# x + alpha * fx: flat chunks instead of partition-major rows, and a first store that waits for an addition

## The chip, the cores and the metric

The kernel runs on one core of a Trainium2 chip. The metric is device time in microseconds of one execution, lower is better. The core has a VectorE (DVE in the profile) that does all the arithmetic here, a SyncE (SP) that issues DMA transfers in order, and 16 DMA engines that carry them out. On-chip memory (SBUF) has 128 partitions; HBM is the memory outside.

## The reference

```python
# x, fx: (512, 32, 640) bfloat16; alpha: (1,) bfloat16
def reference(x, fx, alpha):
    return x + alpha * fx
```

There are 10,485,760 elements in each of x, fx and out, 20.97 MB each, so 62.92 MB must cross between HBM and SBUF: 41.94 in and 20.97 out.

## The kernel before

Each tensor is seen as 128 rows, one for each partition, of 81,920 elements (160 KiB) that lie together in HBM. A row is counted in 160 units of 512 elements (1 KiB). A transfer takes a range of units of all 128 rows.

There is one buffer, `buf`, of 207 units a partition, too small for x and fx together (320). The tables `F` and `X` say at which unit of `buf` a piece of fx or of x lies: `(64, 96, 160)` in `F` puts the units 64 to 96 of fx at place 160. Places are used again: an addition overwrites x with the sum, after which the place of its fx is free for a later load. So a load waits for the additions that free its place, and these wait for earlier loads.

The order is written out by hand in `PLAN`, one step a line, and a loop at the end (lines 128 to 131) walks through it:

- `f i` and `x i` load a piece of fx or x (`load_f`, line 88; `load_x`, line 92), issued on SP;
- `a` brings alpha to all partitions (`alpha_to_lanes`, lines 110 to 118): a two-byte load, a matmul with ones, a copy;
- `m a b` multiplies units a to b of fx by alpha in place (`multiply`, line 97, VectorE);
- `t a b` adds: x becomes x + alpha * fx in place (`total`, line 104, VectorE);
- `s i` stores a piece (`store`, line 108), issued on SP.

Each engine takes its steps in the order of the plan. Waits between engines are put in where places of `buf` overlap, and a step that waits holds up what follows on its own engine. All transfers go through one queue, SP's, and the 16 DMA engines carry them out in that order. The first store comes last but two in the plan, but depends only on additions of units 0 to 64, long done when SP reaches it; so it is issued directly behind the last load of x (`x 3`). At the end (lines 133 to 135) SP waits for everything but the last store, and the program's end for that one.

Of the kernel before, what the change touches and what calls it, by code (L numbers as in the profile page):

```python
# [1 line left out]

# [4 lines left out]

ACT = mybir.ActivationFunctionType
ALU = mybir.AluOpType
F32 = mybir.dt.float32  # L10
BF16 = mybir.dt.bfloat16

K = 512
P = 128


F = [(0, 8, 96), (8, 64, 104), (64, 96, 160), (96, 128, 128), (128, 160, 175)]
X = [(0, 64, 0), (64, 96, 64), (96, 128, 96), (128, 160, 143)]
S = [(0, 64), (64, 128), (128, 160)]
N = 160  # L20
ALL = 207

PLAN = """
f 0
f 1
a
x 0
f 2
x 1
m 0 64  # L30
t 32 64
t 0 32
f 3
x 2
m 64 96
t 79 96
f 4
t 64 79
m 96 128
t 111 128  # L40
x 3
t 96 111
m 128 160
t 128 160
s 0
s 1
s 2
"""


@with_exitstack
def kernel(
    ctx: ExitStack,
    tc: tile.TileContext,
    x: bass.AP,
    fx: bass.AP,
    alpha: bass.AP,
    out: bass.AP,
):
    nc = tc.nc  # L60
    xv = x.flatten_outer_dims().rearrange("(p n) d -> p (n d)", p=P)
    fxv = fx.flatten_outer_dims().rearrange("(p n) d -> p (n d)", p=P)
    ov = out.flatten_outer_dims().rearrange("(p n) d -> p (n d)", p=P)
    assert xv.shape[1] == N * K

    consts = ctx.enter_context(tc.tile_pool(name="consts", bufs=1))
    psum = ctx.enter_context(tc.tile_pool(name="psum", bufs=1, space=bass.MemoryType.PSUM))
    whole = ctx.enter_context(tc.tile_pool(name="whole", bufs=1))
    ctx.enter_context(tc.manual_schedule())

    sync = mybir.DependencyInfo(mybir.DependencyClass.Sync, mybir.DependencyReason.DATA)
    buf = whole.tile([P, ALL * K], x.dtype, name="buf")
    done = []
    lanes = {}

    def units(v, a, b):
        return v[:, a * K : b * K]

    def at(pieces, a, b):

        s, _, h = next(p for p in pieces if p[0] <= a < p[1])
        e, _, g = next(p for p in pieces if p[0] < b <= p[1])
        assert h - s == g - e
        return units(buf, a + h - s, b + h - s)

    def load_f(i):
        a, b, _ = F[i]
        done.append(nc.sync.dma_start(out=at(F, a, b), in_=units(fxv, a, b)))  # L88

    def load_x(i):  # L90
        a, b, _ = X[i]
        done.append(nc.sync.dma_start(out=at(X, a, b), in_=units(xv, a, b)))

    def multiply(a, b):
        term = at(F, a, b)
        done.append(
            nc.vector.tensor_scalar(  # L97
                out=term, in0=term, scalar1=lanes["a_f"][:], scalar2=None, op0=ALU.mult
            )
        )  # L100

    def total(a, b):
        s = at(X, a, b)
        done.append(nc.vector.tensor_tensor(out=s, in0=s, in1=at(F, a, b), op=ALU.add))  # L104

    def store(i):
        a, b = S[i]
        done.append(nc.sync.dma_start(out=units(ov, a, b), in_=at(X, a, b)))

    def alpha_to_lanes():  # L110
        a_1 = consts.tile([1, 1], alpha.dtype, name="a_1")
        done.append(nc.sync.dma_start(out=a_1[:], in_=alpha[None, :]))  # L112
        ones = consts.tile([1, P], alpha.dtype, name="ones")
        nc.vector.memset(ones[:], 1.0)  # L114
        a_ps = psum.tile([P, 1], F32, name="a_ps")
        done.append(nc.tensor.matmul(a_ps[:], ones[:], a_1[:], start=True, stop=True))  # L116
        lanes["a_f"] = consts.tile([P, 1], F32, name="a_f")
        nc.vector.tensor_copy(out=lanes["a_f"][:], in_=a_ps[:])  # L118

    does = {  # L120
        "f": load_f,
        "x": load_x,
        "a": alpha_to_lanes,
        "m": multiply,
        "t": total,
        "s": store,
    }
    for step in PLAN.split("\n"):
        if step:
            what, *of = step.split()  # L130
            does[what](*map(int, of))

    rest = nc.sync.nop(nofuse=True)
    for i in done[:-1]:
        tc.add_manual_dep(rest.ins, i.ins.name, sync, reason="all but the last store")


# [1 line left out]
_INS = ['x', 'fx', 'alpha']  # L139
_OUTS = [((512, 32, 640), 'bfloat16')]  # L140


# [23 lines left out]
```

## Time and profile before

| | |
|---|---|
| median of 3 runs | 151.65 us (151.59 to 151.67) |
| the profiled execution | 151.67 us, of which the span from its first to its last instruction is 149.9 us |
| VectorE busy | 65.9 us, 13 instructions |
| DMA engines | 62.92 MB, 420 GB/s over the span, packets take 98.0% of it |

A page gives one execution. "q1 hardware_dynamic" is the queue that SP fills; the share beside it is the time that its packets took, of 16 engines' span. A row of a group of instructions reads: line, engine, operation, output and inputs with their shapes, count, busy time, mean ns of one, idle time before and what ended it. A row of a stretch reads: from and to in us, its length, busy time of each engine (with the count of instructions), the clock granted to TensorE, the DMA engines' mean share, and GB/s. A row of the timeline reads: start, length in us, engine, line, operation; instructions of one kind are merged, and "SPq" marks the issue of a transfer by SP, not the transfer.

### The profile page before, as it was taken

The page shows a single profiled execution, that of the slowest core. Times are in us where ns is not written, and L with a number is a line of the kernel's source. Part 1 is how long each engine was busy: PE and PEld are TensorE (multiplying, and loading weights), DVE is VectorE, ACT ScalarE, POOL GpSimd, SP SyncE. Part 2 cuts the span into 40 slices and gives each one's busy share as a digit, 9 for nine tenths or more (in the row PEclk, how much of TensorE's full clock was granted, in tenths as well). Part 3 has the DMA queues.
Part 4 walks back from the last instruction along what each step waited for, and adds up shares of the span by engine and source line. Part 5 has one row for each costly group of instructions (what it writes and reads, how often), then busy time and mean ns, then how long its engine had stood idle before and what let it go on. Part 6 is the DMA issues. An engine that isn't in the chain of part 4 may idle for free.

```text
span 149.9 us, 84 instructions
## 1 busy us (share of the span) xinstructions
PE 0.2 (0%) x1; PEld 0.1 (0%) x1; DVE 65.9 (44%) x13; POOL 0.2 (0%) x4
## 2 busy tenths in 40 slices
PE   0000000000000000000000000000000000000000
PEld 0000000000000000000000000000000000000000
DVE  0000009930079999999954998309920000000000
POOL 0000000000000000000000000000000000000000
DMA  5979996969899999999999999998998969697994
GB/s 164 606 337 398 490 525 280 560 280 560 376 437 437 428 420 420 420 420 420 428 463 463 437 437 428 420 420 367 472 490 350 560 280 560 280 560 315 455 446 184
DMA packets 1730, 62.92 MB, mean 420 GB/s; under 512 B 194, under 2 KB 194, under 8 KB 194
## 3 DMA queue, kind: packets, MB, share of 16 engines
q1 hardware_dynamic: 1730, 62.92, 98.0%
HBM read 41.94 MB, written 20.97 MB: 420 GB/s over the span
## 4 chain that ended last, share of the span: by engine, by line
DMA 51%; DVE 20%; SPq 1%; issue 0%; DVEq 0%
DMA buf<-in_x_dram 51%; DVE buf L104 20%; SPq L88 1%; SPq L112 0%; DVEq L104 0%
## 5 line engine op out<-in xcount | busy, mean ns | idle before, releaser
L104 DVE TENSOR_TENSOR buf<-buf 128x16384 bf16<-128x16384 bf16 (+2 forms) x7 | 43.5, 6251 | 20.5 <-DMA buf<-in_x_dram 20.5
L97 DVE TENSOR_SCALAR buf<-buf,a_f 128x16384 bf16<-128x16384 bf16 (+1 forms) x4 | 22.2, 5550 | 0.9 <-DMA buf<-in_fx_dram 0.9
L118 DVE COPY a_f<-a_ps 128x1 f32<-128x1 f32 x1 | 0.2, 157 | 21.5 <-PE a_ps L116 21.5
L114 DVE MEMSET ones<- 1x128 bf16 x1 | 0.2, 165 | 0.8 <-PEq L150 0.8
L116 PE MATMUL a_ps<-a,ones 1*128 1x1 bf16 x1 | 0.2, 158 | 22.3 <-DMA a<-in_alpha_dram 22.3
L150 POOL MEMSET const-bfloat16-1.0<- 128x1 bf16 x1 | 0.1, 101 | 0.0
L150 POOL MEMSET const-uint8-127<- 128x1 uint8 x1 | 0.1, 101 | 0.0
L150 POOL MEMSET const-float32-0.0<- 128x1 f32 x1 | 0.1, 98 | 0.2 <-issue 0.2
L150 POOL MEMSET const-float32-1.0<- 128x1 f32 x1 | 0.1, 98 | 0.0
L116 PEld LDWEIGHTS <-ones 1*128 1x128 bf16 x1 | 0.1, 97 | 1.0 <-DVE ones L114 1.0
## 6 DMA issues: line engine op xcount, KB each, us to landing
buf<-in_fx_dram SPq DMA_DIRECT2D x3, 4096.0 KB, 22.0
buf<-in_x_dram SPq DMA_DIRECT2D x3, 4096.0 KB, 21.4
buf<-in_fx_dram SPq DMA_DIRECT2D x1, 7168.0 KB, 21.4
out_dram<-buf SPq DMA_DIRECT2D x1, 4096.0 KB, 39.5
buf<-in_fx_dram SPq DMA_DIRECT2D x1, 1024.0 KB, 4.9
out_dram<-buf SPq DMA_DIRECT2D x2, 49.8
a<-in_alpha_dram SPq DMA_DIRECT2D x1, 0.0 KB
buf<-in_x_dram SPq DMA_DIRECT2D x1, 39.9
```

Source lines behind the costliest of these rows:

```text
L88: done.append(nc.sync.dma_start(out=at(F, a, b), in_=units(fxv, a, b)))
L97: nc.vector.tensor_scalar(out=term, in0=term, scalar1=lanes["a_f"][:], scalar2=None, op0=ALU.mult)
L104: done.append(nc.vector.tensor_tensor(out=s, in0=s, in1=at(F, a, b), op=ALU.add))
L114: nc.vector.memset(ones[:], 1.0)
L116: done.append(nc.tensor.matmul(a_ps[:], ones[:], a_1[:], start=True, stop=True))
L118: nc.vector.tensor_copy(out=lanes["a_f"][:], in_=a_ps[:])
L150: nc = _bacc.Bacc("TRN2", target_bir_lowering=False, num_devices=1)
```

## The change

The unit becomes 128 elements (`K = 128`). Each tensor is now flat and cut into three chunks of 254, 253 and 133 units a partition: a chunk is a contiguous stretch of HBM, within which each partition has a contiguous row of 63.5, 63.25 or 33.25 KiB (`rows` finds a range of units in its chunk). The table entries, the loads and the stores follow the chunks. fx of the first chunk comes in two loads (8 and 55.5 KiB a partition), x of the second in two (the later units first), so there are 8 loads and 3 stores where there were 9 and 3. `buf` keeps its size: 828 units of 128 elements, 207 KiB.

The additions are cut to fit: 8 of them and 3 multiplications, where there were 7 and 4. The last units of the second chunk that are not yet added, 254 to 309, are now added after the last multiplication, in two steps, 254 to 306 and 306 to 309.

`LATE` is new: the store `s 0 254` gets a wait for the addition `t 254 306`, with which it shares no data. SP issues it once that addition is done. The steps of the plan are now told by their units instead of by a number, and `said` keeps the instruction of each step so that the wait can be attached.

```diff
-K = 512
+K = 128
 P = 128
 
-F = [(0, 8, 96), (8, 64, 104), (64, 96, 160), (96, 128, 128), (128, 160, 175)]
-X = [(0, 64, 0), (64, 96, 64), (96, 128, 96), (128, 160, 143)]
-S = [(0, 64), (64, 128), (128, 160)]
-N = 160
-ALL = 207
+CHUNKS = [(0, 254), (254, 507), (507, 640)]
+
+F = [(0, 254, 507), (254, 507, 254), (507, 640, 442)]
+X = [(0, 254, 0), (254, 507, 575), (507, 640, 309)]
+ALL = 828
 
 PLAN = """
-f 0
-f 1
+f 0 32
+f 32 254
 a
-x 0
-f 2
-x 1
-m 0 64
-t 32 64
-t 0 32
-f 3
-x 2
-m 64 96
-t 79 96
-f 4
-t 64 79
-m 96 128
-t 111 128
-x 3
-t 96 111
-m 128 160
-t 128 160
-s 0
-s 1
-s 2
+x 0 254
+f 254 507
+m 0 254
+t 127 254
+x 380 507
+t 0 127
+x 254 380
+m 254 507
+t 442 507
+f 507 640
+t 380 442
+t 309 380
+x 507 640
+m 507 640
+t 254 306
+t 306 309
+s 0 254
+t 507 640
+s 254 507
+s 507 640
 """
+LATE = {"s 0 254": "t 254 306"}
 
 
 @with_exitstack
...
     out: bass.AP,
 ):
     nc = tc.nc
-    xv = x.flatten_outer_dims().rearrange("(p n) d -> p (n d)", p=P)
-    fxv = fx.flatten_outer_dims().rearrange("(p n) d -> p (n d)", p=P)
-    ov = out.flatten_outer_dims().rearrange("(p n) d -> p (n d)", p=P)
-    assert xv.shape[1] == N * K
+
+    def rows(t, a, b):
+
+        flat = t.rearrange("b s d -> (b s d)")
+        s, e = next(c for c in CHUNKS if c[0] <= a and b <= c[1])
+        v = flat[s * K * P : e * K * P].rearrange("(p n) -> p n", p=P)
+        return v[:, (a - s) * K : (b - s) * K]
 
...
+    said = {}
...
     def at(pieces, a, b):
 
         s, _, h = next(p for p in pieces if p[0] <= a < p[1])
         e, _, g = next(p for p in pieces if p[0] < b <= p[1])
         assert h - s == g - e
-        return units(buf, a + h - s, b + h - s)
+        return buf[:, (a + h - s) * K : (b + h - s) * K]
 
-    def load_f(i):
-        a, b, _ = F[i]
-        done.append(nc.sync.dma_start(out=at(F, a, b), in_=units(fxv, a, b)))
+    def transfer(name, out, in_):
+        r = nc.sync.dma_start(out=out, in_=in_)
+        if name in LATE:
+            tc.add_manual_dep(r.ins, said[LATE[name]].ins.name, sync, reason="issue late")
+        return r
 
-    def load_x(i):
-        a, b, _ = X[i]
-        done.append(nc.sync.dma_start(out=at(X, a, b), in_=units(xv, a, b)))
+    def load_f(a, b):
+        return transfer(f"f {a} {b}", at(F, a, b), rows(fx, a, b))
+
+    def load_x(a, b):
+        return transfer(f"x {a} {b}", at(X, a, b), rows(x, a, b))
+
+    def store(a, b):
+        return transfer(f"s {a} {b}", rows(out, a, b), at(X, a, b))
 
     def multiply(a, b):
         term = at(F, a, b)
-        done.append(
-            nc.vector.tensor_scalar(
-                out=term, in0=term, scalar1=lanes["a_f"][:], scalar2=None, op0=ALU.mult
-            )
+        return nc.vector.tensor_scalar(
+            out=term, in0=term, scalar1=lanes["a_f"][:], scalar2=None, op0=ALU.mult
         )
 
     def total(a, b):
         s = at(X, a, b)
-        done.append(nc.vector.tensor_tensor(out=s, in0=s, in1=at(F, a, b), op=ALU.add))
-
-    def store(i):
-        a, b = S[i]
-        done.append(nc.sync.dma_start(out=units(ov, a, b), in_=at(X, a, b)))
+        return nc.vector.tensor_tensor(out=s, in0=s, in1=at(F, a, b), op=ALU.add)
 
...
     for step in PLAN.split("\n"):
         if step:
             what, *of = step.split()
-            does[what](*map(int, of))
+            said[step] = does[what](*map(int, of))
+            done.append(said[step])
```

More of the change, by code (lines that the diff above doesn't have):

```diff
@@ L73 @@
     done = []
+    said = {}
     lanes = {}
-    def units(v, a, b):
-        return v[:, a * K : b * K]
     def at(pieces, a, b):
```

2 lines of the change are left out of this document (1 added, 1 removed).

## The prediction

> **What bounds the kernel now.** I read the page from the top: busy times, the DMA queue, the chain.
>
> ```profile
> span 149.9 us, 84 instructions
> PE 0.2 (0%) x1; PEld 0.1 (0%) x1; DVE 65.9 (44%) x13; POOL 0.2 (0%) x4
> DMA packets 1730, 62.92 MB, mean 420 GB/s; under 512 B 194, under 2 KB 194, under 8 KB 194
> q1 hardware_dynamic: 1730, 62.92, 98.0%
> DMA 51%; DVE 20%; SPq 1%; issue 0%; DVEq 0%
> ```
>
> VectorE, the only engine with real work, is busy for 44% of the span; the DMA engines for 98%. The chain gives DVE 20%, but that is a chain of permissions (an addition frees a buffer, then a load is issued), and a permission costs time only if the DMA queue has run dry when it comes. Whether it ever does is shown by cutting the span at the moments when the first of the 16 DMA engines begins a new transfer. A packet counts where it starts, so each stretch below holds whole transfers: 9.71 us at 432 GB/s is one of 4096 KB.
>
> ```profile
> core 0: us, PE busy (x) PEld busy (x) DVE busy (x) POOL busy (x), PEclk, DMA share, GB/s
> 0.00:1.74 1.74, 0.00 (x0) 0.10 (x1) 0.17 (x1) 0.20 (x4) 1.00 0.00 0
> 1.74:4.76 3.02, 0.00 (x0) 0.00 (x0) 0.00 (x0) 0.00 (x0) 1.00 1.03 355
> 4.76:21.66 16.90, 0.00 (x0) 0.00 (x0) 0.00 (x0) 0.00 (x0) 1.00 1.00 433
> 21.66:40.99 19.33, 0.16 (x1) 0.00 (x0) 8.91 (x2) 0.00 (x0) 1.00 1.00 434
> 40.99:60.35 19.36, 0.00 (x0) 0.00 (x0) 18.34 (x3) 0.00 (x0) 1.00 1.00 433
> 60.35:70.05 9.70, 0.00 (x0) 0.00 (x0) 9.66 (x3) 0.00 (x0) 1.00 1.00 432
> 70.05:79.77 9.72, 0.00 (x0) 0.00 (x0) 6.85 (x2) 0.00 (x0) 1.00 1.00 432
> 79.77:89.48 9.71, 0.00 (x0) 0.00 (x0) 8.61 (x2) 0.00 (x0) 1.00 1.00 432
> 89.48:99.92 10.44, 0.00 (x0) 0.00 (x0) 4.64 (x2) 0.00 (x0) 1.00 1.01 402
> 99.92:119.25 19.33, 0.00 (x0) 0.00 (x0) 8.69 (x1) 0.00 (x0) 1.00 1.01 437
> 119.25:138.57 19.32, 0.00 (x0) 0.00 (x0) 0.00 (x0) 0.00 (x0) 1.00 1.00 433
> 138.57:148.25 9.68, 0.00 (x0) 0.00 (x0) 0.00 (x0) 0.00 (x0) 1.00 1.00 430
> 148.25:149.90 1.65, 0.00 (x0) 0.00 (x0) 0.00 (x0) 0.00 (x0) 1.00 0.01 0
> ```
>
> Loads and stores run at the same 430 to 437 GB/s, whether VectorE is busy or idle. Only four stretches are not at that pace: 1.74 us before the first packet; the first load, 1 MB in 3.02 us where a seventh of the next row's 7 MB takes 16.90 / 7 = 2.41 (a little more in short packets, say 2.45), so 0.57 lost; the last load of x, 10.44 against 9.71, so 0.73 lost; and 1.65 us at the end. The change can win only there. The third is cut again, beside the load before it:
>
> ```profile
> 79.77:87.05 7.28, 0.00 (x0) 0.00 (x0) 6.18 (x2) 0.00 (x0) 1.00 1.01 437
> 89.48:96.76 7.28, 0.00 (x0) 0.00 (x0) 4.64 (x2) 0.00 (x0) 1.00 1.00 432
> 96.76:99.92 3.16, 0.00 (x0) 0.00 (x0) 0.00 (x0) 0.00 (x0) 1.00 1.01 332
> ```
>
> Six packets of each engine (7.28 us) run at full pace; the last two share 3.16 us at 332 GB/s. The engines are occupied then (share 1.01), so this is no empty queue: the packets themselves are slow. VectorE is idle in that stretch. What is particular to it is that the next thing in the queue is a store, issued long before:
>
> ```profile
> 0.73 0.86 SPq L88 DMA_DIRECT2D buf<-in_fx_dram  x2
> 42.02 17.29 DVE L104 TENSOR_TENSOR buf<-buf 128x16384 bf16<-128x16384 bf16 x2 [10.57 <-DMA buf<-in_x_dram]
> 68.46 0.33 SPq L88 DMA_DIRECT2D buf<-in_fx_dram  x1
> 85.59 0.33 SPq L92 DMA_DIRECT2D buf<-in_x_dram  x1
> 86.02 23.96 SPq L108 DMA_DIRECT2D out_dram<-buf  x3
> 90.52 4.49 DVE L97 TENSOR_SCALAR buf<-buf,a_f 128x16384 bf16<-128x16384 bf16 x1 [0.88 <-DMA buf<-in_fx_dram]
> 100.92 8.69 DVE L104 TENSOR_TENSOR buf<-buf 128x16384 bf16<-128x16384 bf16 x1 [5.92 <-DMA buf<-in_x_dram]
> ```
>
> The first store is issued at 86.02, nearly 14 us before its turn. My reading, an inference, is that the engines fetch ahead for the store while the last loads are still coming in, and the loads pay 0.73 us.
>
> **The change, part by part.**
>
> **Layout and sizes.** Rows of 63.5, 63.25 and 33.25 KiB replace 64 and 32 KiB ones. Bytes are the same. The pace depends hardly on row length: 19.33 us for one transfer with 64 KiB rows, two times 9.71 or 19.36 for two with 32 KiB rows, so 0.03 to 0.09 for a transfer of its own. The plan has 8 loads and 3 stores for the 9 and 3 of before: **0.06 won**. Where a row lies in HBM changes too (pitch 63.5 instead of 160 KiB). Every stretch of 32 to 64 KiB rows is at its ceiling already, so I see nothing to gain there; the first load, with its 0.57, might change by up to that, either way. I take 0.
>
> **VectorE work.** Still 13 instructions on the same elements; the row lengths of the groups give the prices:
>
> ```profile
> L104 DVE TENSOR_TENSOR buf<-buf 128x16384 bf16<-128x16384 bf16 x3 | 26.0, 8689 | 16.5 <-DMA buf<-in_x_dram 16.5
> L97 DVE TENSOR_SCALAR buf<-buf,a_f 128x16384 bf16<-128x16384 bf16 x3 | 13.4, 4483 | 0.9 <-DMA buf<-in_fx_dram 0.9
> L104 DVE TENSOR_TENSOR buf<-buf 128x8704 bf16<-128x8704 bf16 x2 | 9.4, 4692 | 4.0 <-DMA buf<-in_x_dram 4.0
> L97 DVE TENSOR_SCALAR buf<-buf,a_f 128x32768 bf16<-128x32768 bf16 x1 | 8.8, 8752 | 0.1
> ```
>
> An addition costs (8689 - 4692) / 7680 = 0.520 ns an element and some 0.16 us fixed; a multiplication 0.261 ns and 0.21 us. A unit of the new plan is 128 elements. The work is hidden as long as each load is issued before the queue runs dry. With 0.0376 us a KiB of row length (2.416 - 1.213 us over 32 KiB, from 19.33 / 8 and 7.28 / 6) and 8 packets an engine, and VectorE starting 1.03 us after the first engine is through (42.02 against 40.99; 90.52 against 89.48):
> - x 380 507 waits for t 127 254: x 0 254 is through at 40.7, the addition (8.6) runs 41.7 to 50.3. The queue holds fx 254 507 until 59.8. x 254 380 follows t 0 127 at 58.9; the queue then lasts to 69.4.
> - fx 507 640 waits for t 442 507 (4.5 us from 70.4): issued at 74.9, queue dry at 78.9, 4.0 us to spare.
> - x 507 640 waits for t 309 380 (4.9 us from 80.0): issued at 84.9, queue dry at 89.0, 4.1 us to spare.
>
> An issue needs 1.01 us to its first packet (0.73 to 1.74), so all four are covered and I cost them at nothing. Before, the last load had 89.48 - 85.59 = 3.9 us and lost nothing in its first 7.28 us. Were one later by over 3 us, the excess would be paid in full. The additional waits on SP and the last addition (9.0 us from 100.1, freeing a store needed at about 137) are covered as well.
>
> **The held store.** It now waits for t 254 306 and is the one transfer not issued ahead. Let T be the first engine's end of fx 507 640, 89.0. VectorE, idle since 84.9, starts m 507 640 at T + 1.03, for 4.483 + 640 x 0.000261 = 4.65; t 254 306 has 6656 elements: 4.692 - 2048 x 0.00052 = 3.63, starting 0.09 before its predecessor's end (two additions of 8.69 take 17.29). It ends at T + 9.22; SP issues at about T + 9.27; the first packet, by 1.01, at T + 10.28. Meanwhile x 507 640 is 8 packets of 1.213 + 1.25 x 0.0376 = 1.26: done at T + 10.09. So there is a **gap of 0.19**. Behind the waiting store on SP stand only the two other stores, not needed for 19 us more, so the wait delays nobody else.
>
> The first store packet also starts into an idle engine, which no row shows. Its price lies between 0 (stores that were queued ahead: 437 GB/s from the first packet) and 0.57 (the first load, from an empty queue, reading HBM). A store reads SBUF, and the store rows are all at pace, so I take the lower part: **0.20**. Below nothing it cannot be, as 430 to 437 is all that any row reaches.
>
> In exchange the last load has nothing behind it to fetch ahead: **0.73 won**, if my inference holds.
>
> Sum: -0.06 - 0.73 + 0.19 + 0.20 = -0.40. The profiled execution took 151.67 (span 149.9, 1.8 around it), 0.02 over the median 151.65. So 151.27 for it and **151.25** for the median, 0.26% faster. About 0.2%, or 0.30 us, is what I count as a difference from no change.
>
> **The rivals.**
>
> *The store arrives in time.* 1.01 us is the delay of the program's very first DMA; every later one was queued behind others, so the trace shows none. The issue itself takes 0.33; any delay under 10.09 - 9.27 = 0.82 closes the gap and hides the start-up. Taking 0.6, the store comes 0.22 early, at the slow stretch's price of 0.73 / 3.16 = 0.23 a us, 0.05. Time: 151.65 - 0.06 - 0.73 + 0.05 = 150.9. Against it: the only row. The Trainium skill, page "DMA: Bandwidth & Descriptors", section "Latency and other measured facts", gives about 600 ns to the first byte for a transfer issued from SP, which by my sum would be this case; the trace's 1.01 agrees only roughly, and if it is counted from the end of the issue (1.01 - 0.33 = 0.68).
>
> *The hold pays for itself.* Start-up from an idle queue costs a store as much as the first load: 0.19 + 0.57 = 0.76 against 0.73 won, with the 0.06: 151.65 - 0.03 = 151.6, no change.
>
> *Slower.* The last two packets are slow for a reason other than the queued store (the reads ending, say). Then the 0.73 stays, and gap and start-up come on top: 151.65 - 0.06 + 0.39 = 152.0. It decides as soon as less than 0.33 of the 0.73 goes away. For it: no row shows a read stream that ends without a store behind it. Against it: the slowness starts two packets before the store, as fetching ahead would. The Trainium skill speaks for this rival (same page, section "Rules for kernel authors"): issue a DMA early and wait for it late, so that its fixed setup is overlapped; the store of before does so and the held one doesn't. By that rule alone the hold can only lose; the 332 GB/s of the stretch ahead of the early store says that early has a price here.
>
> **How the numbers follow.** Forecast 0.50, with a range of 151.05 to 151.45 (start-up 0 to 0.4; a sixth of it above 151.35); store in time 0.17 (150.85 to 151.05); pays for itself 0.14; slower 0.15 (151.95 to 152.1); 0.04 for a layout effect at the first load, half each way. Faster: 0.42 + 0.17 + 0.02 = 0.61; same: 0.08 + 0.14 = 0.22; slower 0.17. The range 150.9 to 152.05 leaves out half of the second case, a third of the slower one and the layout cases, some 0.17.
>
> **What would show it.** Right: stretches at 430 to 437 GB/s through all loads, the one before the first store too (10.1 us for 33.25 KiB rows); the first store issued near 98.3 and its first packet 0.1 to 0.3 us after the last load's end; a span of 149.5. Early store: first packet with no gap, span 149.15. Slower: the last load still at some 332 GB/s in its last two packets and a gap after it. Wrong altogether: an empty queue ahead of x 507 640 or fx 507 640 (a load's first packet over 0.1 us after its predecessor's last), or a pace other than 430 to 437 in the new layout.

## The result and the profile after

The changed kernel takes 150.90 us (median of 5 runs, 150.88 to 151.02); the kernel before, run beside it, 151.59 (151.46 to 151.67). The ratio is 0.9958, with a 95% interval of 0.9944 to 0.9971: 0.69 us less, where 0.40 was forecast. The profiled execution took 150.88 with a span of 149.1.

The page after:

```profile
span 149.1 us, 83 instructions
PE 0.2 (0%) x1; PEld 0.1 (0%) x1; DVE 65.9 (44%) x13; POOL 0.2 (0%) x4
DMA packets 1586, 62.92 MB, mean 422 GB/s; under 512 B 178, under 2 KB 178, under 8 KB 178
q1 hardware_dynamic: 1586, 62.92, 98.0%
```

Beyond the mean rate, 422 GB/s for 420, nothing in it tells where the 0.8 us of the span went: VectorE's time, the bytes and the share of the DMA engines are the same. The stretches tell, cut again where the first DMA engine begins a new transfer (columns as before: from and to, length, the engines' busy times, clock, DMA share, GB/s); the last two rows cut the last load of x after six of its eight packets.

```profile
1.73:4.82 3.09, 0.00 (x0) 0.00 (x0) 0.00 (x0) 0.00 (x0) 1.00 1.10 384
4.82:21.51 16.69, 0.00 (x0) 0.00 (x0) 0.00 (x0) 0.00 (x0) 1.00 0.99 428
78.97:89.03 10.06, 0.00 (x0) 0.00 (x0) 4.98 (x2) 0.00 (x0) 1.00 1.00 433
89.03:99.14 10.11, 0.00 (x0) 0.00 (x0) 8.46 (x3) 0.00 (x0) 1.00 1.00 431
99.14:118.37 19.23, 0.00 (x0) 0.00 (x0) 9.03 (x1) 0.00 (x0) 1.00 1.00 433
118.37:137.51 19.14, 0.00 (x0) 0.00 (x0) 0.00 (x0) 0.00 (x0) 1.00 1.00 433
137.51:147.60 10.09, 0.00 (x0) 0.00 (x0) 0.00 (x0) 0.00 (x0) 1.00 1.00 432
147.60:149.09 1.49, 0.00 (x0) 0.00 (x0) 0.00 (x0) 0.00 (x0) 1.00 0.01 0
89.03:96.60 7.57, 0.00 (x0) 0.00 (x0) 6.57 (x2) 0.00 (x0) 1.00 1.01 436
96.60:99.14 2.54, 0.00 (x0) 0.00 (x0) 1.88 (x2) 0.00 (x0) 1.00 0.96 416
```

The last load, 4256 KB in 10.11 us, is as fast as the load of the same size before it (10.06). Before, it took 10.44 where its neighbour took 9.71. Its last two packets take 2.54 us now, where two of 1.26 would be 2.52. The first store begins at 99.14, directly behind it, and runs at 433 GB/s from its first packet.

The timeline around it, with the issue of the three stores in the last row (98.24 is the first):

```profile
74.89 0.33 SPq L88 DMA_DIRECT2D buf<-in_fx_dram  x1
84.78 0.33 SPq L88 DMA_DIRECT2D buf<-in_x_dram  x1
90.03 4.65 DVE L104 TENSOR_SCALAR buf<-buf,a_f 128x17024 bf16<-128x17024 bf16 x1 [5.28 <-DMA buf<-in_fx_dram]
94.60 3.89 DVE L110 TENSOR_TENSOR buf<-buf 128x6656 bf16<-128x6656 bf16 x2
98.24 11.25 SPq L88 DMA_DIRECT2D out_dram<-buf  x3
```

The first store was issued 0.90 us ahead of its first packet. The single packets in the trace show how closely the two streams meet: the sixteen engines end the load between 99.12 and 99.56 and begin the store between 99.15 and 99.56, so that none of them stands idle for more than 0.1 us.

### The profile page after: what moved, and what is told of

Its sections match the earlier page's. It is cut to its first block, busy times and chain, and to the rows that moved or that the text cites. A ratio compares the mean times of both kernels' runs of the same rounds, so it can differ in the third digit from the quotient of the medians.

```text
span 149.1 us, 83 instructions
## 1 busy us (share of the span) xinstructions
PE 0.2 (0%) x1; PEld 0.1 (0%) x1; DVE 65.9 (44%) x13; POOL 0.2 (0%) x4
## 4 chain that ended last, share of the span: by engine, by line
DMA 51%; DVE 21%; SPq 1%; issue 0%; DVEq 0%
DMA buf<-in_x_dram 51%; DVE buf L110 21%; SPq L88 1%; SPq L114 0%; DVEq L110 0%
## 5 line engine op out<-in xcount | busy, mean ns | idle before, releaser
L110 DVE TENSOR_TENSOR buf<-buf 128x16256 bf16<-128x16256 bf16 (+6 forms) x8 | 43.7, 5488 | 13.6 <-DMA buf<-in_x_dram 13.6
L104 DVE TENSOR_SCALAR buf<-buf,a_f 128x32512 bf16<-128x32512 bf16 (+2 forms) x3 | 22.0, 7330 | 7.2 <-DMA buf<-in_fx_dram 7.2
```

Source lines behind the costliest of these rows:

```text
L104: return nc.vector.tensor_scalar(out=term, in0=term, scalar1=lanes["a_f"][:], scalar2=None, op0=ALU.mult)
L110: return nc.vector.tensor_tensor(out=s, in0=s, in1=at(F, a, b), op=ALU.add)
```

## The experiments

Theory A: a store that is queued behind the last load slows that load's last packets, and the hold prevents it. Theory B: the flat layout does. In the stretches below, the time that two packets of the same size take at full pace is 2.52 us for rows of 33.25 KiB and 2.43 (a third of 7.28) for rows of 32.

### The hold taken out of the changed kernel

```diff
-LATE = {"s 0 254": "t 254 306"}
+LATE = {}
```

> The changed kernel with the wait of the first store taken out (LATE empty), so that the store is issued right behind x 507 640, near 85. Theory A (a store queued behind the last load slows that load's last packets, and the hold is what helps): the last two packets of x 507 640 are slow again, about 0.73 us lost; time 0.65 to 0.75 above the changed kernel, so 151.55 to 151.65, hardly below the kernel before (0.06 to 0.15 for the transfer saved). Theory B (the flat layout is what helps): the time stays at 150.9 and the last load runs at 430 GB/s or more to its end.

Measured: 151.66 us (151.52 to 151.75), ratio to the kernel before 1.0000 (0.9991 to 1.0008). The last load, and its last two packets:

```profile
88.95:99.79 10.84, 0.00 (x0) 0.00 (x0) 8.46 (x3) 0.00 (x0) 1.00 1.00 402
96.52:99.79 3.27, 0.00 (x0) 0.00 (x0) 2.03 (x2) 0.00 (x0) 1.00 0.96 323
```

The slow end is back: 10.84 against 10.11. The layout, the sizes and the transfer saved together make no difference that these runs can tell; the span of the profiled execution, 149.8, is 0.1 below that of before. Packet by packet, nearly all of the loss falls on the last packet of each engine: it takes 1.59 to 2.21 us, the one before it 1.26 to 1.60, where 1.26 is full pace.

### The hold alone, in the old layout

```diff
-t 96 111
 m 128 160
-t 128 160
+t 99 111
+t 96 99
 s 0
+t 128 160
...
+        if i == 0:
+            tc.add_manual_dep(done[-1].ins, said[99, 111].ins.name, sync, reason="issue late")
```

> The kernel before, its layout, sizes and transfers unchanged; only the addition t 96 111 is moved behind the last multiplication and cut into t 99 111 and t 96 99, and the first store waits for t 99 111, so that it is issued near 98.3, 0.9 us ahead of the first engine's end of the last load. Theory A: the 0.73 us goes away and nothing else changes: 150.85 to 150.95 against 151.6, 0.05 to 0.15 above the changed kernel at most. Theory B: no gain, 151.6.

Measured: 151.11 us (150.89 to 151.26), ratio 0.9962 (0.9950 to 0.9974). The last load and the one before it, and then the issue of the stores:

```profile
79.78:89.50 9.72, 0.00 (x0) 0.00 (x0) 4.69 (x1) 0.00 (x0) 1.00 1.00 432
89.50:99.31 9.81, 0.00 (x0) 0.00 (x0) 8.62 (x3) 0.00 (x0) 1.00 0.99 428
```

```profile
98.38 11.06 SPq L111 DMA_DIRECT2D out_dram<-buf  x3
```

10.44 became 9.81. The hold alone accounts for the change: its interval holds the ratio of the whole change, 0.9958. Whether the layout adds the last 0.0004 is below what the intervals tell apart. Theory B falls. The time is above the 150.85 to 150.95 that were expected, 0.2 above the changed kernel's. The store came a little late here: the first engine would end the load at 89.50 + 9.72 = 99.22, and the first packet of the store starts at 99.31, 0.93 us after its issue. Where the rest of the 0.2 lies was not found.

### When the store must come: 3.5 us earlier, 1.1 us earlier, 1.2 us later

Three variants of the changed kernel move the release of the first store:

```diff
-LATE = {"s 0 254": "t 254 306"}
+LATE = {"s 0 254": "m 507 640"}
```

> The changed kernel with the first store waiting for m 507 640 instead, issued near 94.7, 3.5 us earlier than in the changed kernel and 4.4 us ahead of the last load's end. Theory A with a fetch-ahead of two packets (2.5 us): the first packet of the store can be fetched from about 95.6 on, before the slow stretch began in the kernel before, so the whole 0.73 us is lost: 151.6. If the loss grows with the time that the store has been queued: about a quarter or less of it, 151.0 to 151.1. Theory B: 150.9.

```diff
-t 254 306
-t 306 309
+t 254 290
+t 290 309
...
-LATE = {"s 0 254": "t 254 306"}
+LATE = {"s 0 254": "t 254 290"}
```

> The changed kernel with the last additions cut at 290 instead of 306 and the store waiting for t 254 290: issued near 97.2, 1.1 us earlier than in the changed kernel, its first packet possible from 98.0 on (0.85 after the issue, as the late hold showed), while the last load's engines end at 99.1 to 99.6. Theory A with a fetch-ahead of up to two packets: the store can compete during the last packet only, so about 0.2 to 0.4 of the 0.73 is lost: 151.1 to 151.3 against 150.9 for the changed kernel and 151.6 for the early store. If any queued store costs the full price: 151.6. If arriving during the last packet is free: 150.9.

```diff
 t 254 306
+m 254 280
 t 306 309
...
-LATE = {"s 0 254": "t 254 306"}
+LATE = {"s 0 254": "m 254 280"}
```

> The changed kernel with an idle multiplication of 26 units (over spent fx, about 1.08 us) between t 254 306 and the store, which waits for it: issued near 99.25, 1.0 us later. The result is not changed by it. All theories: the DMA engines run dry. If the changed kernel had no slack at all, the time grows by 1.0, to 151.9; each tenth of slack takes a tenth off. From the gap of the first packet the delay from issue to first packet and the start-up of a store from an idle queue are read: by the prediction 1.01 and 0.20, by the rival that the store arrives in time under 0.82 for the two together.

The first, issued at 94.74, takes 151.65 us (ratio 0.9998, 0.9989 to 1.0007). Its issue, and the last two packets of the load:

```profile
94.74 15.60 SPq L88 DMA_DIRECT2D out_dram<-buf  x3
```

```profile
96.58:99.69 3.11, 0.00 (x0) 0.00 (x0) 1.94 (x2) 0.00 (x0) 1.00 1.01 350
```

The second, issued at 97.16, takes 150.88 (ratio 0.9949, 0.9933 to 0.9966), like the changed kernel:

```profile
97.16 12.34 SPq L88 DMA_DIRECT2D out_dram<-buf  x3
```

```profile
96.58:99.10 2.52, 0.00 (x0) 0.00 (x0) 1.89 (x2) 0.00 (x0) 1.00 0.97 419
99.10:118.27 19.17, 0.00 (x0) 0.00 (x0) 9.03 (x1) 0.00 (x0) 1.00 1.00 434
```

The third, issued at 99.42, takes 151.78 (ratio 1.0009, 0.9999 to 1.0018). The middle row of its stretches is an empty queue:

```profile
99.42 10.06 SPq L89 DMA_DIRECT2D out_dram<-buf  x3
```

```profile
96.56:99.10 2.54, 0.00 (x0) 0.00 (x0) 2.50 (x2) 0.00 (x0) 1.00 0.96 416
99.10:100.26 1.16, 0.00 (x0) 0.00 (x0) 0.72 (x3) 0.00 (x0) 1.00 0.01 0
100.26:119.53 19.27, 0.00 (x0) 0.00 (x0) 8.86 (x1) 0.00 (x0) 1.00 1.00 432
```

Early costs the full price by the median, however long the store has stood in the queue: issued at 94.74, 4.4 us ahead of its turn, the kernel takes what the unheld one takes, 151.65 (the stretch shows 3.11 against 3.27). From 97.16 to 98.24, 1.9 to 0.9 us ahead, the issue costs nothing. For 97.16 I had expected 0.2 to 0.4 us; that was wrong: issued then, the store can begin at 98.0 (by the delay of 0.84 us from the late hold, below), when the engines go from the last packet but one to the last, and it slows neither. Where between 4.4 and 1.9 us the price begins was not tried. Late costs what the queue stands empty: 0.9 us in the median against the changed kernel. The gap of 1.16 is that of the engine that was through first; the sixteen end the load between 99.08 and 99.63 and begin the store between 100.27 and 100.42, so the last of them, which sets the end, waited 0.8. The late hold also gives the two sizes that the prediction had to guess: 0.84 us from issue to first packet (99.42 to 100.26), and a start-up of 0.06 (the first packet of the store takes 2.46 us on every engine, the next 2.40).

### What must stand behind the load: a copy within SBUF, a copy within HBM

Both without the hold; the copy is issued behind x 507 640, the first store behind the copy.

```diff
+    def copy_sbuf():
+        return nc.sync.dma_start(out=buf[:, 701 * K : 828 * K], in_=buf[:, 0 : 127 * K])
...
 x 507 640
+c
+s 0 254
```

> The hold taken out, and a copy from SBUF to SBUF (127 units a partition, over sums of the second chunk, which are then wrong in the output) queued between x 507 640 and the first store. It adds its own time, some 10 us, so only the stretches are read. If reading SBUF ahead is what slows the loads that still write to SBUF (theory A1): the last two packets of x 507 640 are slow as ever, 0.65 to 0.75 lost. If it is the turn from reading to writing at HBM (theory A2): x 507 640 runs at full pace to its end, as the copy behind it neither reads nor writes HBM. The copy itself: full pace, 432 GB/s, if the two directions of the SBUF side do not share a limit; half of it if they do.

```diff
+    def copy_hbm():
+        return nc.sync.dma_start(out=rows(out, 507, 640), in_=rows(x, 507, 640))
...
 x 507 640
+h
+s 0 254
```

> The hold taken out, and a copy from HBM to HBM (the third chunk of x straight to out, whose own store is left out, so that chunk is wrong) queued between x 507 640 and the first store. Only the stretches are read. Theory A1 (reading SBUF ahead): x 507 640 runs at full pace to its end, as the copy reads HBM like a load; the slowness may move to the last packets of the copy, or vanish, as those no longer write SBUF. Theory A2 (turn to writing at HBM): the last two packets of x 507 640 are slow.

With the copy within SBUF, the load's last two packets, then the copy:

```profile
96.63:99.68 3.05, 0.00 (x0) 0.00 (x0) 1.89 (x2) 0.00 (x0) 1.00 1.01 357
99.68:109.29 9.61, 0.00 (x0) 0.00 (x0) 8.48 (x1) 0.00 (x0) 1.00 1.00 433
```

With the copy within HBM, the load's last two packets, then the copy, whole and cut after the first two of its seven packets an engine:

```profile
96.61:99.13 2.52, 0.00 (x0) 0.00 (x0) 1.96 (x2) 0.00 (x0) 1.00 1.00 432
99.13:110.96 11.83, 0.00 (x0) 0.00 (x0) 9.02 (x1) 0.00 (x0) 1.00 1.02 368
99.13:102.01 2.88, 0.00 (x0) 0.00 (x0) 1.80 (x1) 0.00 (x0) 1.00 1.02 432
102.01:110.96 8.95, 0.00 (x0) 0.00 (x0) 7.22 (x1) 0.00 (x0) 1.00 1.02 348
```

A copy that touches no HBM slows the load ahead of it by 0.5 us, a little less than the 0.65 to 0.75 expected; a copy that writes HBM, and reads it like a load, doesn't. So it is not the turn from reading HBM to writing it. What the slow cases share is that the transfer behind the load reads SBUF. Nor is it that SBUF can't be read and written at once: the copy within SBUF does both at 433 GB/s. The HBM copy starts at the pace of a load and is slower from its third packet on, 11.83 us in all for the bytes of a load of 10.11. Its own end shows no price for the store behind it: the last packet takes 1.80 us on the median engine, those before it 1.82.

### Two stores among the loads, and a mirrored buffer

First, the whole first store ahead of the last load, not held:

```diff
+s 0 254
 x 507 640
...
-s 0 254
...
+LATE = {}
```

> The hold taken out and the first store moved ahead of x 507 640, so that the queue has load, store, load, store. Theory A: each end of loads with a store queued behind it costs 0.7, so fx 507 640 and x 507 640 both end slowly: 150.9 + 1.4 = 152.3, plus what a load behind a store costs, which nothing has shown yet: 0 to 0.57, the start-up of the first load. If only the last load of all is slow: 151.6 plus that.

Measured: 151.87 us (151.69 to 151.99), ratio 1.0014 (1.0004 to 1.0023). Rows: the last two packets of fx 507 640, ahead of the first store, then of x 507 640, ahead of the second; and the issues.

```profile
86.55:89.85 3.30, 0.00 (x0) 0.00 (x0) 0.00 (x0) 0.00 (x0) 1.00 0.99 320
...
116.59:119.13 2.54, 0.00 (x0) 0.00 (x0) 0.00 (x0) 0.00 (x0) 1.00 0.97 416
```

```profile
75.34 0.43 SPq L88 DMA_DIRECT2D out_dram<-buf  x1
84.87 0.33 SPq L88 DMA_DIRECT2D buf<-in_x_dram  x1
99.50 30.30 SPq L88 DMA_DIRECT2D out_dram<-buf  x2
```

The first turn is slow, the second is not, though its store was issued at 99.50 and stood in the queue for 19 us. Theory A as I held it falls here: it asked for two slow ends and at least 152.3. So does the other case, that only the last load of all is slow. Two things differ at the second turn: its store reads high places of the buffer, and the load comes behind a store itself. The mirrored buffer tests the first:

```diff
-F = [(0, 254, 507), (254, 507, 254), (507, 640, 442)]
-X = [(0, 254, 0), (254, 507, 575), (507, 640, 309)]
+F = [(0, 254, 67), (254, 507, 321), (507, 640, 253)]
+X = [(0, 254, 574), (254, 507, 0), (507, 640, 386)]
...
+LATE = {}
```

> The hold taken out and the buffer mirrored: every place p of a piece becomes the place counted from the other end, and the order of the units within each chunk is turned with it, so that all overlaps and sizes stay. The first store, queued behind x 507 640, now reads places 574 to 828 instead of 0 to 254. In the run with the store ahead of the last load, the second store, which reads high places, did not slow the load ahead of it. Theory P (the place read decides): no slow end here, 150.9. Theory A (any fetch-ahead from SBUF slows a stream of loads): 0.6 to 0.75 lost as with the store unheld, 151.6.

```profile
96.56:99.82 3.26, 0.00 (x0) 0.00 (x0) 2.03 (x2) 0.00 (x0) 1.00 0.96 324
```

151.51 us in one run, and as slow an end as ever: the place doesn't matter. Then the first store in two parts, `s 0 32` and `s 32 254`, none of them held: the small part between the last two loads, and in another kernel 16 packets an engine earlier, behind x 254 380.

```diff
+s 0 32
 x 507 640
+s 32 254
...
-s 0 254
...
+LATE = {}
```

> The hold taken out and the first store cut: s 0 32 (8 KiB rows) goes between fx 507 640 and x 507 640, s 32 254 behind x 507 640; places as in the changed kernel. Theory A as it stood: both loads end slowly, 0.7 each. Theory S (a load that itself comes behind a store is not slowed by the next store, whatever places that reads): fx 507 640 ends slowly, by up to 0.7, x 507 640 at full pace. Theory P: both slow, as both stores read low places.

```diff
 x 254 380
+s 0 32
...
 x 507 640
+s 32 254
...
-s 0 254
...
+LATE = {}
```

> The hold taken out and the first store cut as in the run with the small store between the last loads, but s 0 32 now goes right behind x 254 380, so that 16 packets an engine of loads (fx 507 640 and x 507 640, 20 us) lie between it and the unheld s 32 254. In the runs with a store between the loads only the first turn from loads to a store was slow, not the second, with 8 packets of loads between. Theory O (the price is paid once, at the first store that is fetched ahead of outstanding loads, and the lead so gained stays): x 254 380 ends slowly, by 0.7 to 1.2, x 507 640 ends at full pace; 151.6 to 152.2. Theory R (a load stream long enough brings it back): both end slowly; 152.3 to 152.8.

The small store between the loads: 152.22 us in one run; the ends of fx 507 640 (1.16 us lost, more than the 0.7 that was expected) and of x 507 640, behind which the larger part had stood in the queue since 85.34.

```profile
86.46:90.14 3.68, 0.00 (x0) 0.00 (x0) 0.00 (x0) 0.00 (x0) 1.00 1.00 296
...
100.12:102.65 2.53, 0.00 (x0) 0.00 (x0) 0.00 (x0) 0.00 (x0) 1.00 1.00 431
```

The small store early: 151.91 us (151.65 to 152.01), ratio 1.0018 (1.0009 to 1.0028); the ends of x 254 380 (two packets of 31.5 KiB, 2.39 us at full pace) and of x 507 640, and the issue of s 32 254, at 85.90, long before that load's end.

```profile
76.61:79.83 3.22, 0.00 (x0) 0.00 (x0) 2.47 (x1) 0.00 (x0) 1.00 0.99 311
...
99.90:102.40 2.50, 0.00 (x0) 0.00 (x0) 1.81 (x2) 0.00 (x0) 1.00 1.03 445
```

```profile
85.90 26.81 SPq L89 DMA_DIRECT2D out_dram<-buf  x3
```

In all three the first turn from loads to a store is slow and no later one is, with 8 or 16 packets of loads between: theory O holds, P and R fall. In these kernels the price is paid once, at the first transfer out of SBUF that stands in the queue directly behind loads, be it only 8 KiB a partition.

### One first load

```diff
-f 0 32
-f 32 254
+f 0 254
...
-LATE = {"s 0 254": "t 254 306"}
+LATE = {"s 0 254": "t 254 298"}
```

> A version that might beat the changed kernel: fx 0 254 in one load instead of two (one transfer fewer, 0.06 to 0.1 won), and the last additions cut at 298, the store waiting for t 254 298, so that it is issued near 97.7, half-way between the hold of the changed kernel and the earlier one that cost nothing. If the first load's 0.57 is the wait for the first data and not a matter of its short packets, nothing else changes: 150.8 against 150.9. If long first packets start worse or better, the stretch of the first load shows it, by up to 0.5 either way.

Measured: 151.25 us (150.97 to 151.40), ratio 0.9974 (0.9965 to 0.9983): not the 150.8 expected but slower than the changed kernel's 0.9958 by the medians and with intervals that overlap a little. Fx of the first chunk, the first addition, and the stretch behind the first engine's end of the last store, in this kernel:

```profile
1.73:21.51 19.78, 0.00 (x0) 0.00 (x0) 0.00 (x0) 0.00 (x0) 1.00 1.01 421
```

```profile
41.98 8.63 DVE L109 TENSOR_TENSOR buf<-buf 128x16256 bf16<-128x16256 bf16 x1 [10.49 <-DMA buf<-in_x_dram]
```

```profile
147.44:149.42 1.98, 0.00 (x0) 0.00 (x0) 0.00 (x0) 0.00 (x0) 1.00 0.00 0
```

The changed kernel has the same first row; its first addition:

```profile
41.60 8.63 DVE L110 TENSOR_TENSOR buf<-buf 128x16256 bf16<-128x16256 bf16 x1 [10.17 <-DMA buf<-in_x_dram]
```

The first engine is through at the same time, 21.51, but the next load has landed on all 16 of them 0.38 us later. The single packets show why: in both kernels the sixteen first ones start within 0.5 us, but those of 63.5 KiB end over 0.85 us (4.74 to 5.59), and the engines stay so far apart to the end. With rows of 8 KiB first they are 0.42 apart at 21.51. So the transfer saved brings the first engine's end of the last store forward from 147.60 to 147.44, but the last engine ends at 148.27 instead of 147.90 (the last stretch is 1.98 against 1.49 above), and the slowest sets the end. The moved hold plays no part in it: the last packets of x 507 640 run at full pace here too, 1.26 us. No version tried beats the changed kernel by more than the runs can tell.

## Why the prediction was right, and what it mis-sized

The direction and the place were right, and so was the cause as far as it is shown: the gain is in the last two packets of the last load, and the hold is what brings it. What the held store itself costs was not right, and the time shows it: 150.90 is outside the forecast's own 151.05 to 151.45 and at the very edge of the range that held the rivals too, 150.9. That it is still inside is luck. Point by point:

- **Layout and sizes, 0.06 won.** Not resolved: the layout without the hold stands at 1.0000 (0.9991 to 1.0008), 0.1 us lower in the span of one execution each. Fx of the first chunk loads as it did: 8 MiB in 19.92 us before (1.74 to 21.66), 1/128 less in 19.78 after.
- **Loads in time.** Right: fx 507 640 and x 507 640 were issued at 74.89 and 84.78 (74.9 and 84.9 forecast), and every load behind fx of the first chunk ran at 431 to 434 GB/s without a gap.
- **The 0.73 us.** Right: 10.44 against 9.71 became 10.11 against 10.06.
- **The gap of 0.19.** This step failed. The issue came at 98.24, T + 9.21, as worked out (T + 9.27), and the load's end at T + 10.11 (10.09); but the delay from issue to first packet was 0.90 here, 0.84 in the late hold and 0.93 in the old layout, not the 1.01 of the program's first transfer. Taking the only row for the nearest was the fault. The first engine waited 0.03 us, not 0.19. The sum also took the load's end as one moment; the engines end it over 0.44 us, and in the late hold a gap of 1.16 at the first of them cost 0.9.
- **The start-up of 0.20.** Mis-sized: 0.06 from an empty queue; here the first packet is slower by at most 0.07, and only on some engines.

Without these two terms the sum is 151.65 - 0.06 - 0.73 = 150.86; 150.90 was measured. So the case that came true is the rival in which the store arrives in time, given 0.17 against 0.50. It came true by a hair: its condition, a delay under 0.82, was not met, and no row had shown its 0.6; but the issue came 0.06 earlier than worked out. Its own price for being early, 0.05, was zero too: issued 1.1 us earlier still, nothing is lost.

The rival that ended slower, the load being slow for another reason, is refuted by the hold alone in the old layout (0.9962). The rule that stood beside it, from the Trainium skill, page "DMA: Bandwidth & Descriptors", section "Rules for kernel authors" (to overlap a DMA with compute, issue it early and wait for it late), is not borne out at this place: the store issued early takes 151.66 us, issued 0.9 to 2 us ahead of its turn 150.9. It holds for being late: 1.16 us of empty queue cost 0.9. The Trainium skill's figure on the same page, about 600 ns to the first byte (section "Latency and other measured facts"), lies between the two ways of counting here: 0.84 us from the start of the issue in the late hold, and 0.51 from its end, less the issue's own 0.33.

My inference on the cause was right in part. The trace shows when packets are carried out, not when their data are fetched, so the fetching ahead itself is not shown. Shown is that a transfer which reads SBUF, issued 4.4 us or more ahead of its turn, slows the last two packets of the loads, and that a store issued 1.9 us ahead does not; that a copy which reads HBM does not; and that it happens once. A reading that would fit: suppose that each engine has room for some data fetched but not yet written, that loads leave it partly empty, and that the first transfer out of SBUF fills it at the expense of loads still on their way; once full it stays so, and no later turn pays. With the store held the room would be filled while nothing else is wanted. That is argued, not shown: no run measures such a room, and why it should stay full through 16 packets of loads is open. Whether a store issued from another engine's queue would be as dear was not tried.

## What to carry to other kernels

Where the DMA engines are the bound, cut the span into stretches at the starts of transfers and look for one whose pace differs from its neighbours': the shares of busy time, 98.0% before and after, hid the 0.7 us that this change was worth. In a kernel that loads, then stores, try holding the first store until the last loads are nearly through: 1.9 to 0.9 us before their end was free here, 4.4 us before it was as dear as not holding at all, and 0.3 us after it lost all that the hold had won. The gain comes once in a program, 0.7 us here, and the window is about 1 us wide where it was tried. A price measured at the start of a program (the first issue, the first load) was an upper end here for the same thing later on: 1.01 became 0.84 to 0.93, and 0.57 became 0.06. And the last of the 16 engines sets the end: a gap or a row that is read at the first of them can be off by their spread, at the end 0.3 us in the changed kernel and 0.8 with one first load.

## What the runs showed of the hardware that was not expected

- The turn from loads to a queued store, or to a queued copy within SBUF, costs 0.5 to 1.2 us once, at the first; later turns from loads to a store ran at full pace (2.50 to 2.54 us for two packets).
- A copy within SBUF runs at 433 GB/s, as fast as a load, though it reads and writes SBUF; a copy within HBM of 4256 KB took 11.83 us, 368 GB/s, where a load of that size takes 10.11.
- A first load in rows of 8 KiB, followed by the rest, keeps the 16 engines closer together than one in rows of 63.5 KiB: 0.42 us apart against 0.85, and 0.38 us at the landing of the next load.
